# An attention kernel on one core: the split input is built in the main loop by Pool instead of being stored once and read back, the gates' column is loaded earlier, and the last additions are spread differently

## The chip, the core and the metric

The kernel runs on one core of one Trainium2 chip. Times are device microseconds of one execution, the median over several. The engines are TensorE (PE, with its weight loads as PEld), VectorE (DVE), ScalarE (ACT), GpSimd (POOL) and SyncE (SP); each executes its own instructions in the order in which the program lists them. DMAs are issued from an engine's queue, here mostly SP's, and a queue issues them in order too: a DMA that has to wait holds up those behind it.

## The reference

Two attentions over the same input `x` of 2048 rows and 576 columns are mixed row by row with a gate:

```
g = sigmoid((x * gate_w).sum(-1))
a = attention with 32 heads of 18, each head with its own q, k, v:  softmax(q k^T / sqrt(18)) v, then @ A_wo
b = attention with 32 heads of 18, own q, but one k and one v for all heads,                 then @ B_wo
out = g * a + (1 - g) * b
```

Both softmaxes are over all 2048 keys, in float32. There are 64 heads in all (`NU`), the 32 that share their keys first.

## The kernel before, in words

Each float32 operand is cut into a high part, rounded to the format in which TensorE multiplies in one pass, and a low part, the remainder; a product is three passes (high by high, low by high, high by low). For `x` this gives nine slices of 128 partitions: five high ones, and four low ones. (576 is four and a half times 128; in the fifth slice the lower 64 partitions hold the high part and the upper 64 the low part of the same rows.)

**The lead** (lines 365 to 463 and 1046 to 1119) loads `x` in columns, cuts it into `X["h"]` and `X["l"]`, projects the first five blocks of 128 output rows (`mt` 0 to 4: shared key, gate column, shared value, and the queries of the shared heads), and sends the results to DRAM and back in the layout that the heads want (`qk_d`, `kq_d`; `first_back`, `rows_back`). While the last two blocks are projected in half steps ("A" on the upper 64 rows of the array, "B" on the lower 64), the row maxima of the first head and a half are taken ("x" and "y": an ACT step and a DVE step). All this stands in one string that is written out by hand and that `lead_steps` executes letter by letter: "s" is a block of scores, "m" a block of maxima, "g" one further step of the generator `gates()`, and "0" a store of a part of the split `x` to the DRAM tensor `x_d` (`store_x`; eight stores, four of 1280 KB and four of 1024 KB, half of them issued from SP, half from POOL).

**The gates.** The gate logits leave the projection as one row, are stored into `z_d` by the four columns of block 0, and are loaded back as the tile `z` of 128 x 16. The first "g" issues that load, the second takes the exponentials on ACT (L478, L479), the later ones the reciprocals and the way back to DRAM.

**The main loop** goes over the steps T = 0 to 1023, 16 for each head u. A step has four blocks of scores (a matmul of 128 x 512 each, L705, and the exponential on ACT, L713), the sums of probabilities times values (L720), and the maxima for a head that comes LEAD = 22 steps later (a matmul, L660, and a DVE reduction, L669). `max_rows(u)` collects a head's maxima (DVE, L676 and L678), cuts them into two parts (`split`, L240 and L242; on POOL, for the first two heads on DVE), writes them to `m_d` and loads them into two rows of `qs`, which the scores of that head multiply; this is issued at T = 10 modulo 16, six steps before the head's first score.

**Units** are woven in between: pieces of other products, taken in half steps from a generator. `value_units` (T = 18 to 226) projects the values of the 32 separate heads, 16 blocks of rows in two halves; `row_units` (T = 234 to 738) projects nine blocks of q and k rows in seven columns of 292 or 296, one unit for each eight steps. In both a unit's input is a column of the split `x`, loaded from `x_d` one unit ahead (`load_xr`, `load`). A generator runs up to its next unit when the first half step of that unit is due. `done` of a row unit cuts the result in two on POOL (`both`) and sends it to `qk_d`; after the fourth and the fifth column it also makes differences of keys.

The units' first weights come at T = 2 (`value_units` loads `wv` in four pieces, through the tile `vg` that has two buffers, and POOL cuts them) and at T = 226 (`row_units`).

**The end**: the output projection adds into `oacc`, in `out_proj`. Its last 32 units (16 row blocks of two halves) come after the last head. A unit whose number is in `ON_ACT` leaves PSUM through ACT into a temporary and is added by POOL (L893, L894); the others are added by DVE (L896). Each finished row block is stored, from SP's queue or from ACT's.

Of the kernel before, what the change touches and what calls it, by code (L numbers as in the profile page):

```python
# [156 lines left out]
def gated_mix_kernel(ctx: ExitStack, tc: tile.TileContext, xT, wall, wv, wo, out):  # L157
# [25 lines left out]
    x_d = dram.tile([P, 2 * NKT - 1, S], F32, name="x_d")  # L183
# [11 lines left out]
    ones_r = dram.tile([2, S], F32, name="ones_r")  # L195
    acc = ps_o.tile([P, 512], F32, name="acc")
# [149 lines left out]
    def rows_back():  # L346
# [4 lines left out]
        for b in (MB, SB):  # L351
            back(qs[0], 1, b, 1024, S)
        for x in (0, 1024):
            back(ksb, 0, MB, x, x + 512)
# [110 lines left out]
    def store_x(i, eng):  # L465
        y, c = "hl"[i % 2], i // 2
        cs = slice(512 * c, 512 * c + 512)
        dma(x_d[:, 0:NKT, cs] if y == "h" else x_d[:, NKT:, cs], X[y][:, :, cs], eng)

# [4 lines left out]
    def gates():  # L474
        z = small.tile([P, 16], F32, name="z")
        dma(z, z_d.rearrange("(p f) -> p f", p=P))
        yield
# [54 lines left out]
    def row_units():  # L532

        pool = L["px"]
        XR, WR = [], []

        def cut(c):
            return slice(292 * c, 292 * c + 292 if c < 6 else S)

# [4 lines left out]
        def load_xr(c):  # L544
            XR.append(pool.tile([P, 2 * NKT - 1, 296], F32R, name="xr", bufs=2))
            n = 296 if c == 6 else 292
            dma(XR[-1][:, :, 0:n], x_d[:, :, cut(c)])
# [14 lines left out]
        load_xr(0)  # L562
        W = {NT: next_w(NT)}
        yield
        for mt in range(NT, MT):
            rs = slice(mt * P, (mt + 1) * P)
            first = pool.tile([P, 4, 292], F32, name="rst", bufs=1).rearrange("p c f -> p (c f)")
            for c in range(7):
                x = XR.pop(0)
                if (mt, c) != (MT - 1, 6):  # L570
                    load_xr((c + 1) % 7)
                n = 296 if c == 6 else 292
# [19 lines left out]
    def value_units():  # L592

        pool = L["px"]
        XV = {}

        def load(st_):
            XV[st_] = pool.tile([P, 2 * NKT - 1, P], F32R, name="xv", bufs=2)
            dma(XV[st_], x_d[:, :, st_ * P:(st_ + 1) * P])

        load(0)
        w = [{y: pool.tile([P, NKT, 288], F32R, name=f"vw{y}{hf}") for y in "hl"} for hf in range(2)]

        for hf in range(2):
            src = wv[:, 288 * hf:288 * hf + 288]
            main = src[0:512, :].rearrange("(p k) m -> p k m", p=P)
            for k0, k1 in ((0, 3), (3, 5)):
                t = L["pool"].tile([P, 16, 76], F32, name="vg", bufs=2)
# [7 lines left out]
        for t in vst:  # L616
            nc.gpsimd.memset(t, 1.0)
        yield
        for st_ in range(16):
            if st_ < 15:  # L620
                load(st_ + 1)
# [204 lines left out]
    ON_ACT = (12, 15, 18, 21, 24, 27)  # L826
# [16 lines left out]
    def out_proj(t0, rows, first=False):  # L843
# [18 lines left out]
        for q in range(8):  # L862
# [3 lines left out]
            for s2 in range(2):  # L866
                st_ = 2 * q + s2
                for hf in range(2):
# [4 lines left out]
                    def done(st_=st_, hf=hf, dst=dst):  # L873
                        if fin and st_ == 15:
                            dma(out[st_ * P:(st_ + 1) * P, 288 * hf:288 * hf + 288], dst, nc.sync if hf else nc.scalar)
                        elif fin and hf:
                            dma(out[st_ * P:(st_ + 1) * P, :], oacc[:, st_, :],
                                nc.scalar if st_ in (8, 10, 12) else nc.sync)
# [209 lines left out]
    def lead_steps(ops):  # L1088

        for op in ops.replace(" ", ""):  # L1090
# [10 lines left out]
            elif op == "0":  # L1101
                store_x(stores.pop(0), nc.sync if len(stores) > 3 else nc.gpsimd)
# [6 lines left out]
    stores = [0, 2, 4, 6, 1, 3, 5, 7]  # L1109
# [146 lines left out]
```

## Time and profile before

| what | value |
|---|---|
| median of 3 runs | 2653.23 us (2652.41 to 2655.94) |
| the profiled execution | 2657.2 us, span 2655.4 us, mean granted clock 0.996 |
| busy share of the span | PE 99%, ACT 92%, DVE 90%, POOL 19% |
| POOL busy | 493.1 us in 728 instructions |
| DMA traffic | 321.64 MB, 121 GB/s on average; 249 to 256 GB/s in the first two of 40 slices |

The profile is of one execution. It lists for each engine when it was busy, and for idle time what ended it (an arrow `<-` with the releaser). PE's ends are modelled, so that PE counts as busy almost everywhere; where it really waited shows as idle time ahead of an instruction, as a lower granted clock, or as weight loads that wait. `L163` is the line of the helper `dma`, `L240` and `L242` the two lines of `split`.

### The profile page before, as it was taken

What the parts mean: (1) busy time and instruction counts of PE and PEld (TensorE: products, weight loads), DVE (VectorE), ACT (ScalarE), POOL (GpSimd) and SP (SyncE); (2) the same over time, 40 slices, a digit from 0 to 9 for tenths busy, and PEclk for the clock granted to TensorE, in tenths of its full rate; (3) what the DMA queues carried; (4) which work ended last, traced back from release to release, by engine and by line L of the source; (5) the groups of instructions that cost most, each with busy time, mean ns of one, the idle gap of its engine ahead of it and who ended that gap; (6) DMA issues with size and microseconds to landing.
All of it is one profiled execution on the core that took longest, in us unless ns stands there. A gap on an engine that the chain in (4) does not pass through costs nothing.

```text
span 2655.4 us, 66530 instructions
## 1 busy us (share of the span) xinstructions
PE 2629.4 (99%) x25405; PEld 1420.0 (53%) x25405; DVE 2394.1 (90%) x4575; ACT 2450.1 (92%) x4862; POOL 493.1 (19%) x728
## 2 busy tenths in 40 slices
PE   9899999999999999999999999999999999999998
PEld 7555555455454545555455554545555555545665
DVE  6789999999999999999999999999999989999883
ACT  5789999999999999999999999999999999999887
POOL 3410000110123112312132114121300020112112
PEclk9999999999999999999999999999999999999999
DMA  8722211321454435435555456545532322224312
GB/s 249 256 76 65 63 51 44 86 82 36 119 154 142 128 116 144 147 122 152 159 178 169 149 152 188 172 145 147 158 102 74 106 92 88 82 70 123 111 54 92
DMA packets 216950, 321.64 MB, mean 121 GB/s; under 512 B 55498, under 2 KB 174234, under 8 KB 205250
## 3 DMA queue, kind: packets, MB, share of 16 engines
q1 hardware_dynamic: 199493, 260.17, 33.7%
q0 software_dynamic: 16240, 55.98, 5.7%
q8 instruction: 200, 3.28, 0.5%
q10 hardware_dynamic: 896, 1.23, 0.1%
q14 instruction: 121, 0.98, 0.1%
HBM read 232.20 MB, written 76.33 MB: 116 GB/s over the span
## 4 chain that ended last, share of the span: by engine, by line
PE 96%; DMA 2%; SPq 1%; DVE 1%; ACT 0%; issue 0%; POOL 0%; POOLq 0%; ACTq 0%; DVEq 0%
PE acc L720 38%; PE bank L660 29%; PE bank L705 18%; PE bank L921 10%; SPq L163 1%; PE acc L732 1%; DMA ksb<-kq 0%; PE bank L901 0%; DMA xs<-xT 0%; DMA xsh<-xT 0%; DMA z<-z_d 0%; PE bank L1073 0%; DMA ke<-pdhl 0%; DVE xl L393 0%; DMA wst<-wall 0%
## 5 line engine op out<-in xcount | busy, mean ns | idle before, releaser
L713 ACT ACTIVATE pt<-bank 128x512 f32<-128x512 f32 x4096 | 2145.6, 615 | 121.5 <-PE bank L705 65.8
L669 DVE TENSOR_REDUCE mx<-bank 128x1 f32<-128x512 f32 x3002 | 1886.8, 684 | 127.4 <-PE bank L705 62.9
L705 PE MATMUL bank<-qs,ksb 56*128 56x512 f32 x2688 | 908.8, 425 | 2.6 <-DMA qs<-m_d 2.6
L660 PE MATMUL bank<-ksb,qs 54*128 54x512 f32 x2270 | 811.4, 427 | 0.0
L720 PE MATMUL acc<-pt,vb 128*19 128x256 f32 (+3 forms) x6168 | 554.9, 455 | 0.0
L660 PEld LDWEIGHTS bank<-ksb,qs 54*128 54x128 f32 x2270 | 385.6, 185 | 308.3 <-ACT pt L713 182.8
L720 PE MATMUL acc<-pt,vg 128*19 128x512 f32 (+3 forms) x6120 | 531.8, 447 | 0.0
L705 PEld LDWEIGHTS bank<-qs,ksb 56*128 56x128 f32 x2688 | 442.5, 185 | 160.5 <-DVE mx L669 64.6
L705 PE MATMUL bank<-qs,ksa 56*128 56x512 f32 x1408 | 468.9, 426 | 0.0
L660 PE MATMUL bank<-ksa,qs 54*128 54x512 f32 x1232 | 442.7, 427 | 0.0
L666 DVE CUSTOM_DVE_ANT_0 junk<-bank,xb 128x512 bf16<-128x512 f32 x500 | 342.9, 686 | 32.4 <-PE bank L705 25.1
L663 ACT ACTIVATE xb<-bank 128x512 f32<-128x512 f32 x500 | 291.5, 604 | 18.8 <-PE bank L705 8.7
L660 PEld LDWEIGHTS bank<-ksa,qs 54*128 54x128 f32 x1232 | 210.5, 184 | 137.6 <-ACT pt L713 76.7
L705 PEld LDWEIGHTS bank<-qs,ksa 56*128 56x128 f32 x1408 | 226.2, 185 | 87.1 <-DVE mx L669 38.5
L720 PEld LDWEIGHTS acc<-pt,vg 128*19 128x19 f32 x6120 | 126.5, 98 | 214.6 <-issue 187.0
L720 PEld LDWEIGHTS acc<-pt,vb 128*19 128x19 f32 x6168 | 124.2, 98 | 204.3 <-issue 171.3
L240 POOL CAST rhl<-rst 128x292 fp32r<-128x292 f32 (+2 forms) x81 | 33.9, 419 | 782.0 <-DVE rst L896 704.0
L240 POOL CAST mh<-mt 128x32 fp32r<-128x32 f32 x62 | 13.0, 210 | 890.2 <-DVE mt L678 890.2
L921 PE MATMUL bank<-xr,wrh 64*128 64x292 f32 (+1 forms) x1134 | 168.2, 301 | 0.0
L660 PE MATMUL bank<-kdb,qs 54*128 54x512 f32 x372 | 160.3, 431 | 0.0
L921 PEld LDWEIGHTS bank<-xr,wrh 64*128 64x128 f32 x1134 | 139.6, 186 | 2.8
L921 PE MATMUL bank<-xr,wrl 64*128 64x292 f32 (+1 forms) x567 | 102.6, 294 | 0.0
(161 smaller groups left out, 2064.6 us busy)
## 6 DMA issues: line engine op xcount, KB each, us to landing
xr<-x_d SPq DMA_DIRECT2D x54, 1314.0 KB
qs<-qk SPq DMA_DIRECT2D x366, 144.0 KB
ksa<-qk SPq DMA_DIRECT2D x132, 144.0 KB
qk<-rhl POOLq DMA_DIRECT2D x54, 292.0 KB, 4.5
xr<-x_d SPq DMA_DIRECT2D x9, 1332.0 KB
xv<-x_d SPq DMA_DIRECT2D x16, 576.0 KB
ksb<-qk SPq DMA_DIRECT2D x60, 144.0 KB
qk<-phl POOLq DMA_DIRECT2D x16, 512.0 KB, 4.8
```

The costliest lines, as they stand in the source:

```text
L163: return (eng or nc.sync).dma_start(o, i)
L240: eng_h.tensor_copy(h, src)
L660: nc.tensor.matmul(pm, qs[u % 3][b:b + 54, i * P:(i + 1) * P], k, start=True, stop=True)
L663: nc.scalar.activation(MX["x", u, i], pm, AF.Relu)
L666: nc.vector.tensor_tensor_reduce(junk, pm, MX.pop(("x", u, i)), 1.0, -3e38, op0=OP.add, op1=OP.max, accum_out=MX[u][:, i, c:c + 1])
L669: nc.vector.tensor_reduce(MX[u][:, i, c:c + 1], pm, axis=AX.X, op=OP.max)
L705: nc.tensor.matmul(ps, kst(u)[b:b + 56, i * P:(i + 1) * P], qs[u % 3][b:b + 56, c * 512:(c + 1) * 512], start=True, stop=True)
L713: nc.scalar.activation(pt, ps, AF.Exp, scale=SCALE)
L720: nc.tensor.matmul(acc[32 * j:32 * j + 19, a:b], v_of(u, i), PT[u, i, j][:, a:b], start=(i == 0), stop=(i == 15), skip_group_check=True)
L732: nc.tensor.matmul(acc[32 * j:32 * j + 19, 256 * half + a:256 * half + b], v_of(NU - 1, i), pt[:, x + a:x + b], start=(i == 0), stop=(i == ...
L921: nc.tensor.matmul(u.fp[op][:, 0:u.n], x[b:b + 64], y[b:b + 64], start=(n == 0), stop=(n == last))
```

## The change

- The tensor `x_d` and its eight stores are gone, and with them the "0" in the lead's string; the other letters of the string but the "g" stand in the same order.
- Units get their columns otherwise: `stage(i)` loads the column of `xT` as it is into two temporary tiles (`oih` and `oil`, buffers of the output projection that are idle then), and `cut_x(i)` makes the nine slices from it on POOL: two casts and three subtractions for a row unit's column, a cast and two subtractions for a value block. A column is staged two units ahead and cut one unit ahead.
- The second half of `wv` is staged in `oih` instead of `vg`, so that the four pieces have four buffers; the `x` column of the first value block is cut after the weights.
- The tile `z` is loaded in `rows_back`, after the queries of the first head; `gates()` begins with the exponentials, at the letter that was the second "g".
- In the last part of the output projection the units 12, 14, 16, 18, 20 and 22 leave through ACT and POOL instead of 12, 15, 18, 21, 24 and 27; row block 14 is stored from ACT's queue, and the two halves of block 15 change queues.

```diff
--- before.py
+++ after.py
@@ -180,7 +180,6 @@
     sum_d = dram.tile([NU, S], F32, name="sum_d")
     r_d = dram.tile([NU, S], F32, name="r_d")
     v_d = dram.tile([16, P, H * 19], F32, name="v_d")
-    x_d = dram.tile([P, 2 * NKT - 1, S], F32, name="x_d")
     on_d = [dram.tile([9 * P, S], F32, name=f"on{x}") for x in "hl"]
 
 
@@ -193,6 +192,7 @@
     vb = fixed.tile([P, 16, 19], F32, name="vb")
     ones = fixed.tile([P, 32], F32, name="ones")
     ones_r = dram.tile([2, S], F32, name="ones_r")
+    z = fixed.tile([P, 16], F32, name="z")
     acc = ps_o.tile([P, 512], F32, name="acc")
 
     nc.vector.memset(acc, 0.0)
@@ -350,6 +350,7 @@
         dma(keb[MB:MB + 54, :], ke_d.rearrange("p a f -> (p a) f"))
         for b in (MB, SB):
             back(qs[0], 1, b, 1024, S)
+        dma(z, z_d.rearrange("(p f) -> p f", p=P))
         for x in (0, 1024):
             back(ksb, 0, MB, x, x + 512)
         for b in (MB, SB):
@@ -462,19 +463,11 @@
             if n == 6:
                 WP.append(prep_w(W.pop(0)))
 
-    def store_x(i, eng):
-        y, c = "hl"[i % 2], i // 2
-        cs = slice(512 * c, 512 * c + 512)
-        dma(x_d[:, 0:NKT, cs] if y == "h" else x_d[:, NKT:, cs], X[y][:, :, cs], eng)
-
     xdp = ph1.enter_context(tc.tile_pool(name="xdp", bufs=1, side="right"))
     small = ctx.enter_context(tc.tile_pool(name="small", bufs=1, side="left"))
     g2 = small.tile([P, 2, 16], F32, name="g2")
 
     def gates():
-        z = small.tile([P, 16], F32, name="z")
-        dma(z, z_d.rearrange("(p f) -> p f", p=P))
-        yield
         nc.scalar.activation(g2[:, 0, :], z, AF.Exp, scale=1.0)
         nc.scalar.activation(g2[:, 1, :], z, AF.Exp, scale=-1.0)
         nc.gpsimd.tensor_scalar(g2, g2, 1.0, None, op0=OP.add)
@@ -532,19 +525,40 @@
     def row_units():
 
         pool = L["px"]
-        XR, WR = [], []
+        XR, WR, XS_ = [], [], []
+        total = 7 * (MT - NT)
 
         def cut(c):
             return slice(292 * c, 292 * c + 292 if c < 6 else S)
+
+        def width(c):
+            return 296 if c == 6 else 292
 
         def load_wr(mt):
             WR.append(pool.tile([P, NKT, P], F32, name="wrst"))
             load5(WR[-1], wall[mt])
 
-        def load_xr(c):
+        def stage(i):
+            n = width(i % 7)
+            t = [L["pool"].tile([P, 4, 256], F32, name="xst", tag=f"oi{y}", bufs=2).rearrange("p k f -> p (k f)")
+                 for y in "hl"]
+            t = [t[k][:, 0:(3 - k) * n].rearrange("p (k f) -> p k f", f=n) for k in range(2)]
+            main, rest = xT[0:512, cut(i % 7)].rearrange("(p k) m -> p k m", p=P), xT[512:576, cut(i % 7)]
+            dma(t[0], main[:, 0:3, :])
+            dma(t[1][:, 0, :], main[:, 3, :])
+            for b in (0, 64):
+                dma(t[1][b:b + 64, 1, :], rest)
+            XS_.append(t)
+
+        def cut_x(i):
             XR.append(pool.tile([P, 2 * NKT - 1, 296], F32R, name="xr", bufs=2))
-            n = 296 if c == 6 else 292
-            dma(XR[-1][:, :, 0:n], x_d[:, :, cut(c)])
+            x, n, (t0, t1) = XR[-1], width(i % 7), XS_.pop(0)
+            nc.gpsimd.tensor_copy(x[:, 0:3, 0:n], t0)
+            nc.gpsimd.tensor_copy(x[:, 3:5, 0:n], t1)
+            nc.gpsimd.tensor_tensor(x[:, 5:8, 0:n], t0, x[:, 0:3, 0:n].bitcast(F32), op=OP.subtract)
+            nc.gpsimd.tensor_tensor(x[:, 8, 0:n], t1[:, 0, :], x[:, 3, 0:n].bitcast(F32), op=OP.subtract)
+            last = x[64:128, 4, 0:n]
+            nc.gpsimd.tensor_tensor(last, t1[64:128, 1, :], last.bitcast(F32), op=OP.subtract)
 
         def next_w(mt):
             W = {y: pool.tile([P, NKT, P], F32R, name=f"wr{y}") for y in "hl"}
@@ -559,7 +573,9 @@
             return hl[:, :, 0:n]
 
         load_wr(NT)
-        load_xr(0)
+        stage(0)
+        stage(1)
+        cut_x(0)
         W = {NT: next_w(NT)}
         yield
         for mt in range(NT, MT):
@@ -567,9 +583,12 @@
             first = pool.tile([P, 4, 292], F32, name="rst", bufs=1).rearrange("p c f -> p (c f)")
             for c in range(7):
                 x = XR.pop(0)
-                if (mt, c) != (MT - 1, 6):
-                    load_xr((c + 1) % 7)
-                n = 296 if c == 6 else 292
+                i = 7 * (mt - NT) + c
+                if i + 1 < total:
+                    cut_x(i + 1)
+                if i + 2 < total:
+                    stage(i + 2)
+                n = width(c)
                 b = (0, 292, 584, 876, 512, 0, 808)[c]
 
                 def done(mt=mt, c=c, n=n, b=b, first=first, rs=rs):
@@ -592,20 +611,28 @@
     def value_units():
 
         pool = L["px"]
-        XV = {}
-
-        def load(st_):
-            XV[st_] = pool.tile([P, 2 * NKT - 1, P], F32R, name="xv", bufs=2)
-            dma(XV[st_], x_d[:, :, st_ * P:(st_ + 1) * P])
-
-        load(0)
+        XV, XS_ = {}, []
+
+        def stage(i):
+            t = L["pool"].tile([P, 4, 256], F32, name="xst", tag="oil", bufs=2).rearrange("p k f -> p (k f)")
+            XS_.append(t[:, 0:NKT * P].rearrange("p (k f) -> p k f", f=P))
+            load5(XS_[-1], xT[:, i * P:(i + 1) * P])
+
+        def cut_x(i):
+            x = XV[i] = pool.tile([P, 2 * NKT - 1, P], F32R, name="xv", bufs=2)
+            t, last = XS_.pop(0), x[64:128, 4]
+            split(t, x[:, 0:5], None, nc.gpsimd, nc.gpsimd)
+            nc.gpsimd.tensor_tensor(x[:, 5:9], t[:, 0:4], x[:, 0:4].bitcast(F32), op=OP.subtract)
+            nc.gpsimd.tensor_tensor(last, t[64:128, 4], last.bitcast(F32), op=OP.subtract)
+
         w = [{y: pool.tile([P, NKT, 288], F32R, name=f"vw{y}{hf}") for y in "hl"} for hf in range(2)]
 
         for hf in range(2):
             src = wv[:, 288 * hf:288 * hf + 288]
             main = src[0:512, :].rearrange("(p k) m -> p k m", p=P)
             for k0, k1 in ((0, 3), (3, 5)):
-                t = L["pool"].tile([P, 16, 76], F32, name="vg", bufs=2)
+                t = L["pool"].tile([P, 4, 256], F32, name="wvs", tag="oih", bufs=2) if hf else \
+                    L["pool"].tile([P, 16, 76], F32, name="vg", bufs=2)
                 t = t.rearrange("p a b -> p (a b)")[:, 0:288 * (k1 - k0)].rearrange("p (k f) -> p k f", f=288)
                 dma(t[:, 0:min(k1, 4) - k0, :], main[:, k0:min(k1, 4), :])
                 if k1 == NKT:
@@ -615,10 +642,15 @@
         vst = [pool.tile([P, 16, 19], F32, name=f"vst{i}") for i in range(2)]
         for t in vst:
             nc.gpsimd.memset(t, 1.0)
+        stage(0)
+        stage(1)
+        cut_x(0)
         yield
         for st_ in range(16):
             if st_ < 15:
-                load(st_ + 1)
+                cut_x(st_ + 1)
+            if st_ < 14:
+                stage(st_ + 2)
             x = XV.pop(st_)
             for hf in range(2):
                 yield Unit([(x[:, k if b == "h" else NKT + k, :], w[hf][a][:, k, :]) for a, b, k, _ in PROJ],
@@ -823,7 +855,7 @@
 
     WO = {}
 
-    ON_ACT = (12, 15, 18, 21, 24, 27)
+    ON_ACT = (12, 14, 16, 18, 20, 22)
     SPARE = ['oh', 'ol']
 
     def prep_wo(t0, rows):
@@ -872,10 +904,10 @@
 
                     def done(st_=st_, hf=hf, dst=dst):
                         if fin and st_ == 15:
-                            dma(out[st_ * P:(st_ + 1) * P, 288 * hf:288 * hf + 288], dst, nc.sync if hf else nc.scalar)
+                            dma(out[st_ * P:(st_ + 1) * P, 288 * hf:288 * hf + 288], dst, nc.scalar if hf else nc.sync)
                         elif fin and hf:
                             dma(out[st_ * P:(st_ + 1) * P, :], oacc[:, st_, :],
-                                nc.scalar if st_ in (8, 10, 12) else nc.sync)
+                                nc.scalar if st_ in (8, 10, 12, 14) else nc.sync)
 
                     how = "copy" if first else "pool" if fin and 2 * st_ + hf in ON_ACT else "add"
                     yield Unit(ops, 288, dst, done, how=how)
@@ -1098,24 +1130,21 @@
             elif op == "m":
                 M, c = last_m.pop(0)
                 step_max(*divmod(M, 16), c)
-            elif op == "0":
-                store_x(stores.pop(0), nc.sync if len(stores) > 3 else nc.gpsimd)
             elif op == "g":
                 next(slow[0], None)
             else:
                 lead_max("x" if op == "x" else "y", op == "y")
 
     last_m = [(LEAD + 1, 2), (LEAD + 1, 3)]
-    stores = [0, 2, 4, 6, 1, 3, 5, 7]
     clk.half = STREAM
     begin_units(lead_units())
     lead_steps("AABABABABABxBAABxyABxBAyABxyABxBAyABxyABABxyABABxyABABABxyAB"
-               "ABxyABABxyAgBABxyABABxyABABxyABABYBABxBABABxyABABxyA0BABxyAB"
-               "ABxyABABxyABABYBABxBAABxyABABxyA0gBABxyABABxyABABxyABABYBABx"
-               "BAABxyABABxyA0BABxyABABxyABABxyABABYBABxBAABxyABABxyA0gBABxy"
-               "ABABxyABABxyABABABxyABABxyABABxyA0gBABxyABABxyABABxyABAsABxy"
-               "ABABxsAyABxyA0BBYsBBBsBB"
-               "s0sm0sms")
+               "ABxyABABxyABABxyABABxyABABxyABABYBABxBABABxyABABxyABABxyABAB"
+               "xyABABxyABABYBABxBAABxyABABxyAgBABxyABABxyABABxyABABYBABxBAA"
+               "BxyABABxyABABxyABABxyABABxyABABYBABxBAABxyABABxyAgBABxyABABx"
+               "yABABxyABABABxyABABxyABABxyAgBABxyABABxyABABxyABAsABxyABABxs"
+               "AyABxyABBYsBBBsBB"
+               "ssmsms")
     clk.half = HALF_MM
 
     PLAIN = "mssmsm 4 smsmsm 3 smmssx 3 smmsys 3 mssxysm 3 msxmssm 3 mssysms 3 msssmys 4 msmsms 3 smxssm 3"
```

## The prediction

> **What bounds the kernel now.** I read the busy shares first, then the costliest groups, then the busy times by stage.
>
> ```profile
> PE 2629.4 (99%) x25405; PEld 1420.0 (53%) x25405; DVE 2394.1 (90%) x4575; ACT 2450.1 (92%) x4862; POOL 493.1 (19%) x728
> L705 PE MATMUL bank<-qs,ksb 56*128 56x512 f32 x2688 | 908.8, 425 | 2.6 <-DMA qs<-m_d 2.6
> 72.00:83.40 11.40, 1.05 (x9) 0.64 (x7) 0.51 (x3) 0.88 (x5) 1.03 (x2) 0.72 0.80 264
> 83.40:87.60 4.20, 4.19 (x22) 3.36 (x24) 2.33 (x7) 2.38 (x5) 3.23 (x4) 0.54 0.97 376
> 140.00:142.70 2.70, 0.09 (x3) 0.07 (x2) 0.55 (x1) 1.00 (x3) 2.49 (x4) 0.84 0.04 6
> 142.70:150.30 7.60, 7.60 (x56) 2.94 (x56) 4.27 (x8) 3.78 (x8) 0.00 (x0) 0.61 0.37 116
> ```
>
> TensorE bounds the whole, and the matmuls of the scores waited once in the run for a DMA, 2.6 us. So the main loop is a stream of matmuls whose number the change does not touch; a change of this kind can gain only where PE stands still or is clocked down. The stage rows (columns: length, then busy time and instructions of PE, PEld, DVE, ACT, POOL, then granted clock, DMA share, GB/s) show two such places: PE works 1.05 of 11.4 us before 83.4 and 0.09 of 2.7 us before 142.7, and after each the clock is 0.54 and 0.61 for some microseconds.
>
> **The first hole: the gates' column.** Chain of waits and the timeline:
>
> ```profile
> 82.55 0.22 ACT L478 ACTIVATE g<-z 128x16 f32<-128x16 f32 x1 [10.52 <-DMA z<-z_d]
> 83.41 0.79 PE L1073 MATMUL bank<-ksb,qs 54*128 54x512 f32 x1 [10.36 <-ACT xd L1077]
> 74.09 8.44 DMA z<-z_d
> 55.58 1.09 SPq L163 DMA_DIRECT2D qs<-kq  x2
> 56.71 1.23 SPq L163 DMA_DIRECT2D ksb<-kq  x2
> 68.12 0.23 SPq L163 DMA_DIRECT2D ksb<-ones_r  x1
> 73.02 1.03 SPq L163 DMA_DIRECT2D qs<-kq  x2
> 74.48 4.91 SPq L163 DMA_DIRECT2D x_d<-xh  x3
> ```
>
> ACT stands for 10.52 us at the exponentials of the gates, because `z` is issued at 74.09, behind the loads of `rows_back`, and takes 8.44 us. ACT executes in order, so the lead's evictions queue behind it, the banks stay full and PE stops for 10.36 us. In the change `z` stands in SP's queue between the rows of 55.58 and 56.71. With the same 8.44 us it lands at about 65.1; ACT wants it at 82.55 - 10.52 = 72.0. That is 7 us of cover; if it went, each us late would cost one. The loads behind `z` on SP come some 0.35 us later, which the lead does not notice: the queries of the second head, the next that it wants, are first used at the 33rd "x" of the string, of which 23 stand before this place, and they had landed by 68.12, where SP had waited for a load issued after them. What is late next? The `x` stores, which began at 74.48, are gone, and the evictions themselves, ACT's own pace, are what remains.
>
> So I take off the whole 10.36 us, and the clock's share: 83.4 to 87.6 at 0.54 loses 4.2 x 0.46 = 1.9 us. Together 12.3. Bounds: 0 (`z` late all the same) and 12.3.
>
> **The second hole: the row maxima of the second head.** SP's waits, then the timeline:
>
> ```profile
> SPq L163 <- DMA x_d<-xl: 20.8, 1, 20.8
> 119.85 1.14 SPq L163 DMA_DIRECT2D ksa<-ones_r  x4
> 123.11 14.91 SPq L163 DMA_DIRECT2D vg<-wv  x8
> 127.16 0.19 DVE L242 TENSOR_TENSOR mh<-mt,mh 128x32 fp32r<-128x32 f32 x1
> 138.07 0.59 SPq L163 DMA_DIRECT2D m_d<-mh  x1
> 139.90 1.24 SPq L163 DMA_DIRECT2D qs<-m_d  x2
> 142.66 0.76 PE L705 MATMUL bank<-qs,ksb 56*128 56x512 f32 x1 [2.61 <-DMA qs<-m_d]
> ```
>
> SP stood 20.8 us until the last `x` store had let go of its memory (119.85). Then the four pieces of `wv` took 14.91 us on the queue, since two buffers make the third piece wait until POOL has cut the first. Behind them the maxima, ready at 127.35, were issued at 138.07, 10.7 us late. PE needed the two rows at 142.66 - 2.61 = 140.05. Both causes go: no store holds the memory, and four buffers let SP issue all eight DMAs without POOL. New on SP ahead of the maxima are six loads for two staged columns, about 0.6 us each by the rows above (two DMAs in 1.24 us), 3.6 us. The queue should be free several us before the maxima are ready; from there to PE's need it takes 142.66 - 138.07 = 4.6 us, while 140.05 - 127.35 = 12.7 are there. I take off 2.61, and for the clock 7.6 x 0.39 = 3.0. Together 5.6; bounds 0 and 5.6.
>
> [...]
>
> **The end.**
>
> ```profile
> 2646.75 1.65 DVE L896 TENSOR_TENSOR oacc<-bank,oacc 128x288 f32<-128x288 f32 x4 [0.34 <-PE bank L901]
> 2647.75 0.34 ACTq L163 DMA_DIRECT2D out<-oacc  x1
> 2648.19 0.41 ACT L893 ACTIVATE tmp<-bank 128x288 f32<-128x288 f32 x1 [1.36 <-DVE oacc L896]
> 2648.68 0.79 POOL L894 TENSOR_TENSOR oacc<-tmp,oacc 128x288 f32<-128x288 f32 x1 [0.96 <-ACT tmp L893]
> 2649.49 1.31 SPq L163 DMA_DIRECT2D out<-oacc  x3
> ```
>
> DVE adds the last unit at 2648.40, but unit 27 leaves ACT only at 2648.60, because ACT's queue held a store (2647.75) that waited for POOL. POOL adds until 2649.47, and three stores wait behind that on SP: the last is issued at 2650.80. With the new list units 24 to 31 are all DVE's, four of which took 1.65 us, as fast as PE makes them. The last store then follows DVE's 2648.40 by one issue of 0.34, on ACT's queue: 2648.74. Gain 2.06, taken as 2.1. Bounds: 0 (a bank is late because ACT, which now also issues block 14, falls behind), and 2.7 if the closing follows POOL, whose last addition moves from unit 27 to 22, some 2.7 us earlier.
>
> **What POOL takes over.**
>
> ```profile
> L240 POOL CAST vwh<-vg 128x864 fp32r<-128x864 f32 x2 | 1.8, 903 | 19.0 <-DVE mx L669 17.5 <-DMA vg<-wv 1.5
> L240 POOL CAST vwh<-vg 128x576 fp32r<-128x576 f32 x2 | 1.3, 658 | 0.4 <-DMA vg<-wv 0.4
> L242 POOL TENSOR_TENSOR vwl<-vg,vwh 128x864 fp32r<-128x864 f32 x2 | 4.1, 2046 | 0.2
> L242 POOL TENSOR_TENSOR rhl<-rst,rhl 128x292 fp32r<-128x292 f32 x54 | 43.8, 812 | 4.4
> L240 POOL CAST wrh<-wrst 128x640 fp32r<-128x640 f32 x9 | 6.5, 728 | 26.4 <-DMA wrst<-wall 26.4
> L242 POOL TENSOR_TENSOR ol<-ot,oh 128x512 fp32r<-128x512 f32 x32 | 41.1, 1284 | 6.0 <-DMA onl<-ol 3.9
> L787 POOL TENSOR_TENSOR sm<-sm,gt 128x128 f32<-128x128 f32 x1 | 0.5, 457 | 14.6 <-DVE sm L784 14.6
> L744 DVE COPY oe<-acc x63: 691/692/694, 150.5 to 2601.3; 128x512 f32<-128x512 f32 x63
> ```
>
> A row column costs a cast of 876 elements (0.90), one of 584 (0.66), subtractions of 876 (2.05) and twice 292 (0.81 each): 5.2 us, 63 times, 329 us. A value block costs 0.73 + 1.28 + 0.46 = 2.5 us, 16 times, 40 us. POOL goes from 493 to about 860 us, a third of the span. A unit has half a head: the 62 heads between the two copies of the L744 row give 2450.8 / 62 / 2 = 19.8 us. So 5.2 of 19.8 us fits, and a column is cut a whole unit before PE wants it; staged another unit earlier, its load, of 748 KB in four DMAs (2.4 us on SP), has as long. Cost on the path: 0. The cover is those 19.8 us; if POOL were full, PE would wait for a column, up to 5.2 us a unit.
>
> Who waits behind POOL is the cut of the maxima. The narrowest case I found is head 31 (its first score is the matmul of L705 after 31 x 64):
>
> ```profile
> 1311.38 0.22 POOL L240 CAST mh<-mt 128x32 fp32r<-128x32 f32 x1
> 1315.30 1.26 SPq L163 DMA_DIRECT2D qs<-m_d  x2
> 1319.98 0.39 PE L705 MATMUL bank<-qs,ksb 56*128 56x512 f32 x1
> ```
>
> The second load is issued at about 1315.94, lands some 2.1 us later (as at 140.54 to 142.66), and PE uses it at 1319.98: 2 us to spare. But the order in the program helps: the maxima are issued at T = 10 modulo 16, a unit's first half step comes 11 to 16 blocks of scores into its eight steps, so each `cut_x` follows that head's maxima or precedes them by half a head, where POOL sat idle. I take 0, with bounds of -1 (half the DMA traffic per column) and the rival below.
>
> **The sum.** 12.3 + 5.6 + 2.1 = 20.0 us. The profiled execution took 2657.2 us, so 2637.2 for a profiled one; it lies 4.0 above the median, and I take the same 20.0 off the median: 2633.2.
>
> **The rivals.**
>
> *POOL late before the maxima* (slower). If `cut_x` came to lie directly in front of the cut of the maxima in the heads that have little to spare, each would lose 5.2 - 2.0 = 3.2 us and, after such a hole, the clock's 3.0 as above, 6.2 us. It decides from four such heads on to cancel the gain; if a seventh of the 45 heads between T = 18 and 738 were like head 31, six or seven, it is 6.5 x 6.2 = 40, and 2653.2 - 20 + 40 = 2673. For it: POOL's third of the span and head 31. Against: the order above. Chance 0.08.
>
> *DVE blocked by POOL at the second hole.* The first two heads' maxima are cut on DVE. In the lead such a cast met a POOL subtraction and took 1.02 us instead of the 0.18 of the other:
>
> ```profile
> 92.20 1.29 POOL L242 TENSOR_TENSOR phl<-pst,phl 128x512 fp32r<-128x512 f32 x1
> 92.52 1.02 DVE L240 CAST mh<-mt 128x32 fp32r<-128x32 f32 x1
> 94.44 0.49 PE L1073 MATMUL bank<-ksb,qs 54*128 54x512 f32 x1 [1.04 <-DVE mx L1083]
> ```
>
> It ended with POOL's, and PE then waited 1.04 us. In the change POOL cuts weights and the first column around the second head's maxima. Cast and subtraction could each wait for a 2.05 us subtraction: 4.1 less gain, 2637.3. [...] Chance 0.2.
>
> *The second hole stays*, because SP is held by something else that lets go of the lead's memory late: 20.0 - 5.6 = 14.4, 2638.8. Chance 0.1.
>
> *The change doesn't do what it says for `z`*: its load must wait on SP for the last store into `z_d`, and lands late with all loads behind it; 12.3 comes back, 2645.5. Against: that store is issued 5 us earlier. Chance 0.04.
>
> *The lead shrinks, yet something unseen in the main loop returns it*: within 0.2% of before, 0.05.
>
> **How the numbers follow.** The forecast has what is left, 0.53. A measurement of this kernel tells 0.2%, 5.3 us, from no change. All cases but the first and the last rival are faster by more: 0.87; within: 0.05; slower: 0.08. The range runs from 2629 (the upper bounds of the end and of POOL, and a cast in the lead that no longer meets POOL: 1.7, 2.5 with its clock) to 2641, which takes in the blocked DVE and the hole that stays.
>
> **What would show it.** Right: no idle time of ACT at L478 and a granted clock of 1.0 from 60 to 150 us; scores without a wait for `m_d`; the first copy of L744 at about 132.6 instead of 150.5, and the last some 18 us earlier too; POOL near 860 us; the last store issued about 2 us after the last matmuls' bank instead of 3. Wrong: waits of L705 for `qs<-m_d` or of L921 for POOL in the main loop, or a distance between the first and the last copy that is over 2451 us by more than 2.

## The result and the profile after

The changed kernel takes 2638.92 us (median of 4 runs, 2638.23 to 2639.09), the kernel before in the same comparison 2653.67 us (4 runs, 2652.41 to 2655.94). The ratio is 0.9943, 95% interval 0.9926 to 0.9960: 14.75 us, 0.56%, faster. The prediction was 2633.2, range 2629 to 2641, faster.

The two profiled executions took 2657.2 and 2639.09 us, 18.1 apart. The starts of the matmuls of the scores (L705 before, L737 after) say in which stage the time went:

| from the span's start, us | before | after | gain so far |
|---|---|---|---|
| first score of head 0 | 100.96 | 88.43 | 12.5 |
| first score of head 1 | 142.66 | 128.63 | 14.0 |
| first score of head 2 | 186.54 | 169.81 | 16.7 |
| last score of head 63 | 2631.85 | 2615.10 | 16.75 |
| end of the span | 2655.41 | 2637.30 | 18.1 |

So the lead gave 12.5 us, the way over to the main loop 4.2, the main loop nothing (2445.31 and 2445.29 us between the third row and the fourth), and the end 1.4.

The head of the page of the changed kernel, and the costliest PE group:

```profile
span 2637.3 us, 67281 instructions
...
PE 2625.7 (100%) x25405; PEld 1418.5 (54%) x25405; DVE 2393.5 (91%) x4575; ACT 2449.8 (93%) x4862; POOL 851.4 (32%) x1087
...
L737 PE MATMUL bank<-qs,ksb 56*128 56x512 f32 x2688 | 908.3, 425 | 0.0
```

The number of matmuls is the same, and those of the scores no longer wait (0.0 in the last column). POOL went from 493 to 851 us, and in the list of PE's waits none is for a column that POOL cuts. ACT no longer stands at the exponentials of the gates (82.55 before, with 10.52 us of idle time):

```profile
71.73 0.22 ACT L471 ACTIVATE g<-z 128x16 f32<-128x16 f32 x1
```

The two places of the lead by stage (length, busy time and count of PE, PEld, DVE, ACT, POOL, then clock, DMA share, GB/s):

```profile
72.00:83.40 11.40, 10.35 (x85) 8.64 (x85) 10.24 (x32) 9.67 (x20) 8.80 (x10) 1.00 0.62 204
83.40:87.60 4.20, 4.20 (x38) 3.60 (x38) 3.87 (x11) 3.60 (x7) 3.72 (x4) 1.00 0.20 58
...
124.00:132.00 8.00, 8.00 (x89) 4.32 (x85) 7.52 (x17) 7.86 (x17) 0.00 (x0) 1.00 0.13 39
```

PE works 10.35 of the 11.4 us in which it worked 1.05 before, the clock stays at 1.0, and across head 1's first score (128.63) PE is never idle. SP's queue, with the load of `z` and the maxima of the second head:

```profile
53.99 1.27 SPq L163 DMA_DIRECT2D z<-z_d  x1
...
93.13 1.62 SPq L163 DMA_DIRECT2D ksa<-ones_r  x4
...
96.03 2.31 SPq L163 DMA_DIRECT2D vg<-wv  x4
98.39 3.76 SPq L163 DMA_DIRECT2D wvs<-wv  x4
102.19 4.80 SPq L163 DMA_DIRECT2D xst<-xT  x6
116.14 0.33 SPq L163 DMA_DIRECT2D m_d<-mh  x1
117.64 1.23 SPq L163 DMA_DIRECT2D qs<-m_d  x2
```

SP gets to the key rows of ones at 93.13 instead of 119.85, and has been free for 9 us when the maxima come, at 116.14 instead of 138.07.

### The profile page after: what moved, and what is told of

It is laid out like the page before. It is cut to its first block, busy times and chain, and to the rows that moved or that the text cites. A ratio compares the mean times of both kernels' runs of the same rounds, so it can differ in the third digit from the quotient of the medians.

```text
span 2637.3 us, 67281 instructions
## 1 busy us (share of the span) xinstructions
PE 2625.7 (100%) x25405; PEld 1418.5 (54%) x25405; DVE 2393.5 (91%) x4575; ACT 2449.8 (93%) x4862; POOL 851.4 (32%) x1087
## 3 DMA queue, kind: packets, MB, share of 16 engines
q14 instruction: 125, 1.02, 0.1%
## 4 chain that ended last, share of the span: by engine, by line
PE 99%; DVE 0%; DMA 0%; ACT 0%; POOL 0%; issue 0%; ACTq 0%; SPq 0%; DVEq 0%
PE acc L752 38%; PE bank L692 29%; PE bank L737 18%; PE bank L953 10%; PE bank L278 2%; PE acc L764 1%; PE bank L933 1%; PE bank L1105 0%; DMA xsh<-xT 0%; POOL oacc L926 0%; DVE mx L701 0%; DVE mh L240 0%; PE bank L1007 0%; DVE junk L1115 0%; PE bank L326 0%
## 5 line engine op out<-in xcount | busy, mean ns | idle before, releaser
L737 PE MATMUL bank<-qs,ksb 56*128 56x512 f32 x2688 | 908.3, 425 | 0.0
L737 PEld LDWEIGHTS bank<-qs,ksb 56*128 56x128 f32 x2688 | 441.3, 184 | 158.5 <-DVE mx L701 64.8
L737 PE MATMUL bank<-qs,ksa 56*128 56x512 f32 x1408 | 468.2, 426 | 0.0
L737 PEld LDWEIGHTS bank<-qs,ksa 56*128 56x128 f32 x1408 | 225.9, 184 | 86.9 <-DVE mx L701 37.6
L558 POOL TENSOR_TENSOR xr<-xst,xr 128x876 fp32r<-128x876 f32 (+1 forms) x63 | 130.6, 2073 | 0.0
```

What stands on the lines that cost most here:

```text
L558: nc.gpsimd.tensor_tensor(x[:, 5:8, 0:n], t0, x[:, 0:3, 0:n].bitcast(F32), op=OP.subtract)
L737: nc.tensor.matmul(ps, kst(u)[b:b + 56, i * P:(i + 1) * P], qs[u % 3][b:b + 56, c * 512:(c + 1) * 512], start=True, stop=True)
```

## The experiments

**The kernel before once more**, unchanged, one execution (2655.39 us). 

> The kernel before, unchanged, for a second profile of it. Theory A (the time of the kernel before varies because the first hole, which a DMA ends, varies, and the profiled execution shown had a long one): PE's idle time at the first hole differs from 10.36 us, somewhere in 6 to 10.4, the total moves with it, and the 2451 us from the first to the last copy of the accumulators stay within 1 us. Theory B (the main loop varies): the hole is 10.4 again and the stretch between the copies differs by 2 us or more.

PE's two holes in this execution:

```profile
83.40 0.79 PE L1073 MATMUL bank<-ksb,qs 54*128 54x512 f32 x1 [10.85 <-ACT xd L1077]
...
141.98 0.59 PE L705 MATMUL bank<-qs,ksb 56*128 56x512 f32 x1 [1.78 <-DMA qs<-m_d]
```

The first is 0.5 us longer than in the profile shown, the second 0.8 shorter, and behind the second the clock was at half for 3.4 us, not 6.8, which is worth another 1.7. That is 2.0 us in all; the execution was 1.8 shorter. From head 2 to the last score it took 2445.25, as in both other profiles. Theory A had the right kind of cause but the wrong hole: the first was longer, and the second with its clock made the difference. So between these two executions of the kernel before, it is the two holes that vary, which end with DMAs, and not the main loop.

**`z` alone.** The kernel before, its stores kept, with the load of `z` moved as in the change:

```diff
 def rows_back():
+    dma(z, z_d.rearrange("(p f) -> p f", p=P))     # behind the loads of qs[0]
 def gates():
-    dma(z, z_d.rearrange("(p f) -> p f", p=P))     # and the first "g" of the string
-    yield
```

> The kernel before, with the load of z alone moved to its new place; the stores of the split x stay. Theory A (z was late by its place in SP's queue): no idle time of ACT at the exponentials, the lead 12.3 us shorter than in the profile of before (first score at about 88.6), the second hole still there with 2 to 3 us; timed 9 to 12 us under the kernel before, 2641.5 to 2645. Theory B (z was late through the traffic of the stores, wherever it stands): ACT still waits 5 us or more at the exponentials, and the gain is under 5 us.

It took 2658.55 us against 2656.18 (ratio 1.0009, 1.0000 to 1.0018; 11 and 21 runs): nothing gained. The profile is of the fastest of the 11 (2654.86). Neither expectation held as a whole. The first hole was gone and ACT did not wait at the exponentials, but a new one of 12.15 us stood ahead of the very first score. SP's queue, then that matmul, then the piece of the chain that ends in it:

```profile
72.72 5.02 SPq L163 DMA_DIRECT2D x_d<-xh  x3
80.92 2.20 SPq L163 DMA_DIRECT2D m_d<-mh  x1
```
```profile
100.62 0.76 PE L704 MATMUL bank<-qs,ksb 56*128 56x512 f32 x1 [12.15 <-DMA qs<-m_d]
```
```profile
80.92 13.27 DMA m_d<-mh
94.20 0.61 SPq L163
94.86 5.62 DMA qs<-m_d
```

The maxima of the first head, 32 KB, were written behind three stores of `x` of 1280 KB each that SP had issued just before, and their way took 13.27 us, the load of the two rows 5.62 more. In the kernel before these stores (issued from 74.48 on) ran while everybody stood waiting for `z`, and the maxima were cut only after that: their write was issued at 93.79, and the load that follows it at 95.24, 1.45 us later.

**The stores alone.** The changed kernel with the load of `z` back in `gates()`, so that all of the change is in but that:

```diff
 def rows_back():
-    dma(z, z_d.rearrange("(p f) -> p f", p=P))
 def gates():
+    dma(z, z_d.rearrange("(p f) -> p f", p=P))
+    yield
```

> The changed kernel, with the load of z back at its old place, at the first g; no stores of x. Theory A (place): z is issued at about 73, behind 864 KB of queries, and lands 5 to 8 us later; ACT waits 5 to 9 us, and with the clock the kernel is 6 to 11 us over the changed one, 2645 to 2650. Theory B (traffic of the stores): without them z lands in 2 to 3 us, ACT waits 3 to 4 us, and the kernel is at most 5 us over the changed one.

2652.07 us against 2656.18 (ratio 0.9985, 0.9976 to 0.9993; 11 and 21 runs), 13 us more than the whole change took in the other comparisons. This is theory A, somewhat beyond its upper ends. The chain of waits, and ACT:

```profile
73.41 8.69 DMA z<-z_d
```
```profile
82.13 0.22 ACT L472 ACTIVATE g<-z 128x16 f32<-128x16 f32 x1 [10.13 <-DMA z<-z_d]
```

With no store anywhere the load of `z` still took 8.69 us from here and ACT stood for 10.13. So it is the place of the load in SP's queue, behind the loads of `rows_back`, that made the first hole, and not the stores. The two runs together (differences from 2656.18):

| | `z` late | `z` early |
|---|---|---|
| stores of `x` | 0 | +2.4 |
| no stores | -4.1 | -17.1 |

(The last field is the run that follows, of the same comparison; it has the whole change but the four buffers. The lower row holds the rest of the change too, of which the end is worth 1.4 us by the profiles.) The parts do not add: each of the two waits covers the other.

**Two buffers for the value weights.** The changed kernel with all four pieces of `wv` in `vg`, as before:

```diff
-t = L["pool"].tile([P, 4, 256], F32, name="wvs", tag="oih", bufs=2) if hf else \
-    L["pool"].tile([P, 16, 76], F32, name="vg", bufs=2)
+t = L["pool"].tile([P, 16, 76], F32, name="vg", bufs=2)
```

> The changed kernel, with the four pieces of wv in two buffers again. Theory A (what made the maxima late on SP was the wait for the last store of x; without it the two buffers are in time): the second head's maxima are issued within 1 us of their cut, no idle time at the scores; within 1 us of the changed kernel. Theory B (the four buffers were needed): the maxima are again issued 3 us or more late behind the weights, PE waits, and the kernel is 3 to 6 us over the changed one.

2639.12 us (5 runs, 2638.80 to 2641.16), ratio to before 0.9939 (0.9927 to 0.9951): the same as the change. SP:

```profile
95.28 17.17 SPq L163 DMA_DIRECT2D vg<-wv  x8
112.49 3.86 SPq L163 DMA_DIRECT2D xst<-xT  x6
116.44 0.53 SPq L163 DMA_DIRECT2D m_d<-mh  x1
```

The eight loads take 17 us on the queue (15 in the kernel before), and the six new ones stand behind them; but since SP starts 27.8 us earlier than it did (123.11), the queue is free 0.1 us before the maxima are issued. With the stores gone, the four buffers are no part of the gain; they leave the queue free for 9 us ahead of the maxima instead of 0.1. Whether four buffers alone, with the stores kept, would have closed the second hole was not tried.

**The changed kernel again**, on another chip than the four runs above: 2639.07 us (5 runs, 2639.02 to 2641.72) against 2655.31, ratio 0.9942 (0.9929 to 0.9954). 

> The changed kernel, unchanged, on the chip of the next three. 2638 to 2641 us, 14 to 18 under the kernel before: where executions of the kernel before differ by several us (its holes end with DMAs), those of this one should not.

The gain, 16.2 us, is as expected, the steadiness only in part: four of the five executions lie within 0.8 us, and the fifth is 2.6 us above the median. No profile of it is kept.

**The second head's maxima cut on POOL**, ahead of the weights (the loads stay at T = 2, the cuts of weights and first column wait until T = 10):

```diff
-max_rows(u, nc.gpsimd if T > 16 else nc.vector)
+max_rows(u, nc.gpsimd)
-when(2, lambda: begin_units(value_units()))
+values = value_units()                       # with a yield between its loads and its cuts
+when(2, lambda: next(values)); when(10, lambda: begin_units(values))
```

> The changed kernel, with the second head's maxima cut on POOL, in its queue ahead of the cutting of the value weights. Theory A (DVE stood 1.28 us behind POOL's subtractions there, and PE behind DVE): the steps T = 10 and 11 take 4.2 us instead of 5.4, and from the third head on all is 1.2 to 1.4 us earlier than in the changed kernel. Theory B (DVE had that much room): no change within 0.3 us. Against both: if the value weights come too late for the first value unit, PE waits there, several us.

2637.10 us (5 runs, 2636.95 to 2637.28) against 2639.07 for the changed kernel in the same comparison. In the changed kernel the place looks like this (POOL, DVE, PE):

```profile
113.40 1.42 POOL L242 TENSOR_TENSOR vwl<-wvs,vwh 128x576 fp32r<-128x576 f32 x1
...
114.42 1.01 DVE L240 CAST mh<-mt 128x32 fp32r<-128x32 f32 x1
...
114.76 0.63 POOL L644 MEMSET vst<- 128x304 f32 x2
115.35 0.71 POOL L240 CAST xv<-xst 128x640 fp32r<-128x640 f32 x1
115.47 0.64 DVE L242 TENSOR_TENSOR mh<-mt,mh 128x32 fp32r<-128x32 f32 x1
...
116.77 0.49 PE L692 MATMUL bank<-ksb,qs 54*128 54x512 f32 x1 [0.66 <-DVE mx L701]
```

and with the cut on POOL:

```profile
114.01 0.21 POOL L240 CAST mh<-mt 128x32 fp32r<-128x32 f32 x1 [16.24 <-DVE mt L714]
114.30 0.25 POOL L242 TENSOR_TENSOR mh<-mt,mh 128x32 fp32r<-128x32 f32 x1
114.64 0.91 POOL L240 CAST vwh<-vg 128x864 fp32r<-128x864 f32 x1
```

The two cuts take 0.46 us instead of 1.65, DVE is free for the reductions on which PE waits, and PE's hole is gone: head 2 begins at 167.92 instead of 169.31 us.

**The first head's maxima on POOL too**: `max_rows(0, nc.gpsimd)` in the lead. 

> The changed kernel, with the first head's maxima cut on POOL too, in the lead. Theory A (PE's idle time of 1.05 us there is DVE waiting for POOL's subtraction): the idle time goes, first score up to 1 us earlier. Theory B (POOL is behind there and delivers the maxima 2 us later, with 2.9 us to spare): the idle time goes, but the first score waits for the maxima, 0 to 2 us.

2638.03 us (5 runs, 2636.99 to 2639.96), ratio to before 0.9936 (0.9924 to 0.9949). PE's hole of 1.05 us behind the cast is gone, but the cut now waits its turn on POOL (it begins at 81.78, on DVE in the same comparison at 79.43), and another 0.3 us of idle time appears ahead of the first score, which begins at 87.57 instead of 87.88. Between the two expectations: 0.3 us in the profile. (The median is 1.0 lower, but the runs scatter over 3 us.)

**The end: two stores back from ACT to SP**, in the changed kernel:

```diff
-nc.scalar if st_ in (8, 10, 12, 14) else nc.sync)
+nc.scalar if st_ in (12, 14) else nc.sync)
```

> The changed kernel, with the stores of row blocks 8 and 10 on SP's queue instead of ACT's. Theory A (at the end ACT's queue held evictions behind stores that wait for POOL, and so PE ran out of banks): the idle time of PE at unit 29, 0.35 us, goes, and the span is 0.4 to 0.6 us shorter than the changed kernel's. Theory B (the banks are short for another reason): the idle time stays and the time is the same within 0.2 us.

2637.83 us (5 runs, 2637.04 to 2640.52), ratio 0.9936 (0.9923 to 0.9950). From the last score to the span's end it is 21.11 us instead of 22.20, more than the 0.4 to 0.6 that theory A had. The changed kernel, POOL, ACT with its queue and PE, in order of time:

```profile
2627.82 1.56 POOL L926 TENSOR_TENSOR oacc<-tmp,oacc 128x288 f32<-128x288 f32 x2 [0.98 <-ACT tmp L925]
...
2629.41 0.34 ACTq L163 DMA_DIRECT2D out<-oacc  x1
2629.85 0.41 ACT L925 ACTIVATE tmp<-bank 128x288 f32<-128x288 f32 x1 [1.81 <-PE bank L933]
...
2630.32 0.41 PE L933 MATMUL bank<-woh,qs 128*128 128x288 f32 x1 [0.35 <-ACT tmp L925]
```

and with the two stores on SP:

```profile
2626.87 0.41 ACT L925 ACTIVATE tmp<-bank 128x288 f32<-128x288 f32 x1 [0.38 <-POOL oacc L926]
```

In the changed kernel a store in ACT's queue (2629.41) waits for POOL's addition, which ends at 2629.38; the last eviction by ACT waits behind that store, and PE for the bank. (The row of the eviction names PE, whose matmuls it also needs; that the store held it shows by its coming earlier without the store.) With the stores on SP the last eviction comes 2.2 us earlier, counted from the last score (12.57 us behind it instead of 14.75), and PE does not wait.

**The end as before**, in the changed kernel:

```diff
-ON_ACT = (12, 14, 16, 18, 20, 22)
+ON_ACT = (12, 15, 18, 21, 24, 27)     # and the queues of the stores as before
```

> The changed kernel, with the end as in the kernel before: units 12, 15, 18, 21, 24 and 27 through ACT and POOL, and the old queues of the last stores. Theory A (the new end is worth the difference of the two profiles, from the last score to the end of the span 23.56 us before and 22.20 after): 23.5 us there again, 1.3 to 1.4 us over the changed kernel. Theory B (the closing follows the last store alone): 24 us or more, 2 us over.

2640.48 us (4 runs, 2639.22 to 2643.32), ratio 0.9945 (0.9930 to 0.9961). That is 1.4 over the changed kernel's 2639.07, the size of theory A, but not at the place: in its profile the stretch from the last score to the end is 22.52 us: not the 23.57 of the kernel before, and only 0.3 above the changed kernel's 22.20. The other 1.05 us of the difference to the kernel before are in POOL's closing. The three `DRAIN` instructions of POOL in the program's last line (shortest, median, longest in ns), in the kernel before, in this one, and in the changed one:

```profile
L1252 POOLq DRAIN  x3: 40/102/5988, 2648.6 to 2655.1; - x3
```
```profile
L1281 POOLq DRAIN  x3: 40/102/4925, 2632.6 to 2638.0; - x3
```
```profile
L1281 POOLq DRAIN  x3: 40/102/4937, 2630.3 to 2637.0; - x3
```

With the stores of `x` in the program, half of which POOL issued, the long one takes 5.99 us (in the run of `z` alone too), without them 4.93 (5.13 with two of the last stores moved to SP). In the kernel before and in this one the span ends 0.8 us after it, so 1.06 us of the gain at the end comes with the stores, and 0.3 from the new list. Whether it is POOL's four stores that count, or another thing that went with them, was not tried.

**POOL's room.** The changed kernel with the two casts and the two larger subtractions of each row column made twice:

```diff
-            nc.gpsimd.tensor_copy(x[:, 0:3, 0:n], t0)          # and the three that follow
+            for _ in range(2):
+                nc.gpsimd.tensor_copy(x[:, 0:3, 0:n], t0)
```

> The changed kernel, with the two casts and the two large subtractions of a row unit's column made twice: POOL gets 4.4 us more for each of 63 columns, some 280 us, 1130 in all. Theory A (POOL has room, a column is cut a unit ahead): no idle time of PE for a column, the main loop (second head's first score to the last score) longer by less than 3 us, and that only where a head's maxima had under 5 us to spare. Theory B (POOL is near its limit in the row units): PE waits for columns, several us in each of the nine blocks, 30 us or more.

2639.51 us (4 runs, 2639.26 to 2640.46), ratio 0.9940 (0.9926 to 0.9953): not to be told from the changed kernel.

```profile
PE 2627.1 (100%) x25405; PEld 1420.2 (54%) x25405; DVE 2394.6 (91%) x4575; ACT 2449.9 (93%) x4862; POOL 1120.4 (42%) x1339
```

269 us more on POOL, and from head 2 to the last score 2445.95 us instead of 2445.3: theory A.

**The rival's case, brought about.** Eleven additions, as long together as a column's cut, stand on POOL right ahead of the cut of the maxima of heads 3 to 47:

```diff
 def max_rows(u, ...):
+    if 3 <= u < 48:
+        for _ in range(11):
+            nc.gpsimd.tensor_tensor(dum, dum, dum, op=OP.add)     # 128 x 128
```

> The changed kernel, with eleven small additions on POOL, 5.1 us, directly ahead of the cut of the maxima of heads 3 to 47; they work on a tile of their own. This is the rival of the prediction, a column's cut in front of the maxima. Theory A (only a head whose maxima are late already loses; in the changed kernel heads 17, 24, 31, 38 and 45 have 3.7 to 5.1 us to spare, the others 7 to 9): up to 1.4 us in each of three to five heads, and half clock of 3.4 us behind such a hole, 2 to 12 us in all. Theory B (each head loses, as POOL has no idle time there): 45 heads times some us, 50 us or more.

2647.01 us (5 runs, 2645.40 to 2648.92), ratio 0.9967 (0.9955 to 0.9979), 7.9 over the changed kernel. POOL's timeline, PE's longest wait, and the sum of such waits (total, times, longest):

```profile
1843.95 5.18 POOL L716 TENSOR_TENSOR dum<-dum 128x128 f32<-128x128 f32 x11
...
1853.97 0.46 PE L742 MATMUL bank<-qs,ksa 56*128 56x512 f32 x1 [2.23 <-DMA qs<-m_d]
```
```profile
PE bank L742 <- DMA qs<-m_d: 4.1, 4, 2.2
```

Four of the 45 heads wait, 4.1 us in all; the clock falls once, behind the longest, for 3.4 us, which costs another 1.7. From head 2 to the last score it takes 2452.31 us, 7.0 more; the remaining 1.2 us are not traced. Theory A, then.

**The best version**: the maxima of both first heads on POOL, and the two stores on SP. 

> The changed kernel with three of the edits that gained: the stores of row blocks 8 and 10 on SP, the second head's maxima on POOL ahead of the value weights, the first head's on POOL too. If their gains add (1.1 + 1.9 + 0.7), 3.5 us under the changed kernel, 2635 to 2636; if they share a wait, less, but not under 1.9.

2636.93 us (5 runs, 2636.34 to 2637.96), ratio to before 0.9930 (0.9917 to 0.9942). The span is 2634.9 us, 2.4 under the changed kernel's; the three gains (2.0, 1.0 and 1.2 by their own medians) do not add up, and the second head's maxima alone come within 0.2 us of it. The 2635 to 2636 that was expected was missed. In the profile head 2 begins 2.0 us earlier and the end is 1.1 us shorter than in the changed kernel's, but the main loop takes 0.7 more; why is open.

## Why the prediction was right, and where its terms were off

**The first hole** (12.3 predicted, 12.5 measured) went as described: the load lands in time, ACT does not stand, the evictions' own pace remains, and the clock stays up. But the step counts it as the work of `z` alone, and that is wrong: `z` alone gave nothing. The prediction asked what is late next, found that the stores "are gone", and left it there. What would have been late next, with the stores, was the first head's maxima behind them: with `z` early the first score comes at 100.62 with the stores and at 87.70 to 88.43 without. The 12.5 us need both, the move of `z` and the removal of the stores. Whether the stores could have stayed, issued behind the maxima or all from POOL, was not tried.

**The second hole** (5.6 predicted, 4.2 measured). Nothing waits for the maxima any more. The missing 1.4 us are the rival of the blocked DVE, which had a chance of 0.2 and a price of up to 4.1: the steps T = 10 and 11 together take 5.42 us (4.15 in the kernel before), and 4.11 with the cut on POOL, 1.3 less. The price was too high because the two DVE instructions met only the last part of POOL's work: the cast ended with the memsets that follow POOL's subtraction (115.43 and 115.39), the subtraction with POOL's cast (116.11 and 116.06). They took 1.01 and 0.64 us instead of 0.18 and 0.19. The prediction's row showed this for a cast; that the subtraction, too, could be held up was an estimate. With the cut on POOL both take 0.46 us together, and the 1.3 us are gone. Of the two causes that the step named for the late maxima, the removal of the stores was enough by itself; after it the two buffers no longer counted.

**The end** (2.1 predicted, 1.4 measured). From the start of the last matmul to the span's end the change saved 1.99 us (7.80 to 5.81). That this is the predicted 2.06 is luck: the prediction put it down to the list alone, and 1.06 of it is POOL's shorter closing. Against it stands what the step named as the bound of 0 and did not take, that a bank is late because ACT also issues a store: 0.35 us of PE, and 0.6 until the last matmul.

**POOL** (about 860 us predicted, 851 measured; main loop 0, measured 0). A column by form:

```profile
L556 POOL CAST xr<-xst 128x876 fp32r<-128x876 f32 x54 | 49.5, 916 | 28.5 <-DMA xst<-xT 28.4
...
L557 POOL CAST xr<-xst 128x584 fp32r<-128x584 f32 x54 | 36.5, 677 | 1.4 <-DMA xst<-xT 1.4
...
L558 POOL TENSOR_TENSOR xr<-xst,xr 128x876 fp32r<-128x876 f32 x54 | 111.7, 2069 | 0.0
...
L559 POOL TENSOR_TENSOR xr<-xst,xr 128x292 fp32r<-128x292 f32 x54 | 43.8, 812 | 0.0
L561 POOL TENSOR_TENSOR xr<-xst,xr 64x292 fp32r<-64x292 f32 x54 | 43.8, 811 | 4.2
```

5.29 us, where 5.2 was taken. The first copy of the heads' results and the last stand 2450.9 us apart, as they did (2450.8); the first came 16.6 us earlier, where 18 was forecast, by what the second hole gave less:

```profile
L776 DVE COPY oe<-acc x63: 690/692/694, 133.9 to 2584.8; 128x512 f32<-128x512 f32 x63
```

The cover held with room: twice the cut cost nothing that could be measured. The order in POOL's queue was as described, too; at head 31 the column's cut stands right behind that of the maxima:

```profile
1293.91 0.25 POOL L242 TENSOR_TENSOR mh<-mt,mh 128x32 fp32r<-128x32 f32 x1
1294.12 0.90 POOL L556 CAST xr<-xst 128x876 fp32r<-128x876 f32 x1
```

The slower rival was priced far too high. It had six or seven heads at 6.2 us; with POOL's work ahead of all 45, four heads lost, and 7 us in all. The holes were 1.0 us each on average, where 3.2 was reckoned: the prediction took the 2 us that head 31 had to spare in the kernel before, and in the changed kernel, reckoned in the same way, it has 5. And it gave each hole the clock's price of the second one; only one of the four brought half clock.

**The sum** was 20.0 against 18.1 in the two profiles. The step that missed most is the last one, "the same 20.0 off the median". The profile shown of the kernel before lay 3.5 us above the median of the comparison. Its holes were long in that execution, but the first experiment shows only 2.0 us of this; the rest is not shown. The changed kernel has no such holes, and its profile lies 0.2 from its median. So a gain that consists of those holes is smaller at this median: 14.75. The median of the kernel before differs between comparisons as well: it was 2656.18, 2655.31 and 2655.91 in the later ones, and the gain 17.1 (with two buffers) and 16.2 in the two that allow it. How much of the miss is the first comparison's low median, over four runs, stays open.

## What to carry to other kernels

A stall that is removed is worth what the next one leaves: look what waits behind it on the same queue, and, where two changes hide each other's gain, try each alone before crediting either. Ask of a variable stall how long it was in the profile at hand, and take it off that execution, not off the median. When an engine with much room takes over work, look less at its busy share than at what stands directly behind the new work in its queue: here 269 us more on POOL were not to be told from none, and 5.2 us right ahead of the cut of each head's maxima cost 7.9.

## What the runs showed of the hardware that was not expected

**Half clock lasted 3.4 us or two to four times as long, and a short hole sometimes brought it and sometimes did not.** Ahead of the closing it lasted 10.24 us (76.99 to 87.23) and 6.83 us (141.85 to 148.67) in the kernel before, 3.4 us behind the second hole of the first experiment, behind the hole shown here and in the rival's case, and about 13.7 us with `z` alone (mean clock 0.63 from 88 to 100 us and 0.51 from 100 to 105). In the kernel before the clock fell while PE stood: 3.9 us into the hole of 10.36 us, and 1.8 us into that of 2.61. Stages behind 1.25 us of idle time (changed kernel, `z` late, between 127.90 and 130.70) and behind 1.79 (`z` alone, between 141.40 and 143.20):

```profile
130.70:134.10 3.40, 3.40 (x30) 1.34 (x22) 2.75 (x5) 2.24 (x5) 2.24 (x3) 0.50 0.20 48
134.10:140.00 5.90, 5.90 (x58) 2.98 (x56) 5.19 (x11) 5.17 (x11) 0.00 (x0) 1.00 0.17 53
```
```profile
143.20:150.00 6.80, 6.80 (x70) 3.11 (x74) 5.88 (x11) 5.61 (x12) 0.00 (x0) 1.00 0.39 130
```

The shorter idle time halved the clock, the longer did not; another of 1.78 did (the first experiment), another of 1.25 did not (the rival's case, between 1577.50 and 1585.00, clock 1.00). In the changed kernel 1.05 us between 76 and 88 did not either. So the length of a hole alone did not decide; what did is not shown, and no run moved a hole to test it.

**A small DMA behind large ones on its queue took long**: with `z` alone the 32 KB of the maxima took 13.27 us behind 3.8 MB; in the changed kernel, on a queue that was free, the load that follows them was issued 1.5 us after them (116.14 to 117.64). With `z` alone the DMA engines were fully busy from 88 to 100 us (share 1.02, 389 GB/s); whether that or the place in the queue held the maxima was not told apart.
